# A linear-attention block with an MLP behind it: packets of two tokens for three loads, one chunk's inverse split by parity, and a new order of all steps

## The chip, the cores and the metric

The kernel runs on one core of one Trainium2 chip. The metric is the device time of the whole program in microseconds (us), the median over several runs; the profile is of one execution. The core has a tensor engine (PE, matrix products), a vector engine (DVE), a scalar engine (ACT), GpSimd (POOL) and SyncE (SP), which here only issues transfers. PEld in the profile is the loading of weights into PE.

## What is computed

```python
k_n = k / (np.linalg.norm(k, axis=-1, keepdims=True) + 1e-06)
for t in range(S):
    y[:, :, t] = einsum('bhd,bhde->bhe', q[:, :, t], state)
    v_old = einsum('bhde,bhd->bhe', state, k_n[:, :, t])
    state += beta[:, :, t] * einsum('bhd,bhe->bhde', k_n[:, :, t], v[:, :, t] - v_old)
x = y.transpose(0, 2, 1, 3).reshape(B, S, H * D)
xn = (x - mean(x)) / sqrt(var(x) + 1e-06) * g_ln
out = x + maximum(xn @ w_ch1, 0) @ w_ch2
```

There are 4 batches, 8 heads, 768 tokens and a head width of 48, all in FP32; the MLP goes from 384 to 1536 and back. The state starts at zero.

## The kernel before

**Tiling.** The 768 tokens are worked in 12 chunks of 64. Inside a chunk the recurrence is solved at once: the Gram matrix of the keys is made (`gram`, L786), a unit triangular matrix built from it and the norms is inverted, and the state is taken from chunk to chunk by `recur` (L967). Behind each chunk comes its part of the MLP (`mlp`, and for chunk 0 `by_halves`, L1313). The 32 heads of all batches stand side by side: two batches (index `e`) on the two halves of the 128 partitions, and the other index (`g`) and the heads in the free dimension.

**Chunk 0's inverse** (`first_inverse`, L648) is on PE and DVE, by doubling of blocks: after a first masked step, five steps, each a product E (L720), a masked copy on DVE (L727), a product Z (L737), transposes on DVE (L685) and copies on ACT (L679), for two groups of heads `g`. Then `recur(0)` makes u (product L996, scaled on DVE, L1001), y (L1020), the layer norm and its turn (L1092), and the MLP of chunk 0 begins (L1322).

**The other chunks' inverses** (`rows_inverse`, L822) are on DVE, row after row: for each row j one product of `n * w` elements (L856) and one subtraction (L863), with n = j + 1 and w = 31 - j, on blocks of 32 tokens. Chunk 1 stands alone on 64 partitions; later chunks go in pairs on 128. The Gram matrix goes to DRAM (`gd`) and comes back as rows (`gb`); the finished inverse goes by DRAM (`xd`) to `xts`. `join` (L879) puts two blocks of 32 together on PE.

**Loads.** `load_padded` (L445) reads queries of chunks 0 and 1 with one token of one head (48 numbers, 192 bytes) in a packet, into 64 columns per head of `tb[1]`; `load_raw` (L456) does so for keys, with the halves swapped for odd heads. `first_kt` (L561) turns 128x128 pieces with PE transposes (the profile names them L568) and copies them out on ACT (L573). `TURNED` (L225) says up to which chunk keys have swapped halves; `key_half` (L757) answers to it. The norms of a chunk are gathered as 4-byte packets of the Gram diagonal (`norms`, L920).

**Weights** come as 64-bit numbers through ACT's queue (`fetch`) and are made FP32 by ACT, DVE and POOL (`convert`, L514 to L542).

**Order.** Every step is put on a list by `add`; a table of numbers, `ORDER` (from L59), written out in full, says in which order they are issued. Each engine takes its steps strictly in that order, and so do the transfers on the SP and ACT queues among each other. A step waits on the semaphores of what it needs; all that stands behind it on its engine waits with it. A `z` in the table is a filler, a product of zeros by the unit matrix (L1511); `fill` (L553) issues wide products of zeros. The costs and due times that the calls of `add` carry have no effect on what is issued.

## Time and profile before

| | |
|---|---|
| median of 3 runs (lowest to highest) | 509.65 us (509.59 to 509.78) |
| the profiled execution | 506.83 us |
| its span, first to last instruction | 505.1 us |
| mean granted PE clock | 0.973 |
| packets on SP's queue | 189920, 40.58 MB |

A busy share says how much of the span an engine had an instruction in work. The clock is the share of full speed that PE was granted; here it is 0.50 or 1.00 for a few us at a time in the first 56 us and 1.00 from there to the end. Idle time before an instruction is put down to what ended it; "issue" means that nothing in the profile explains it. PE's waits before 48 us add up as the prediction tells; after that the longest is 0.4 us (L894, for DVE).

### The profile page before, as it was taken

The numbers are of one execution on the slowest core, as the hardware profiler recorded it, in microseconds if no ns is written. First come the engines' busy times: TensorE is split into PE (matmuls) and PEld (weight loads), VectorE is DVE, ScalarE is ACT, GpSimd is POOL, SyncE is SP. The second block draws the span as 40 slices with busy tenths as digits, with TensorE's granted clock in tenths as the row PEclk, the third lists the DMA queues.
The fourth block names the chain that finished last, engine by engine and source line by source line (L and its number), as shares of the span: only waits on it lengthen the run. The fifth ranks groups of instructions, "written<-read, shape, count | busy, mean of one in ns | idle before, by whom it ended". The sixth has DMA issues, their size and how long they took to land.

```text
span 505.1 us, 22184 instructions
## 1 busy us (share of the span) xinstructions
PE 485.9 (96%) x9606; PEld 445.7 (88%) x9606; DVE 355.2 (70%) x774; ACT 249.0 (49%) x620; POOL 275.7 (55%) x430
## 2 busy tenths in 40 slices
PE   6777999999999999999999999999999999999996
PEld 3666988688988898899999999999999999999996
DVE  9689987997699458886559898478899238143251
ACT  5777772633645434636444544436563347363230
POOL 5464527255754595629893462591642851645643
PEclk9776799999999999999999999999999999999999
DMA  8979896756646676448734434765245412111101
GB/s 173 308 153 187 270 189 79 107 138 133 90 87 106 192 127 114 46 100 205 155 41 64 102 55 153 150 91 87 57 85 136 82 23 58 43 50 46 31 12 31
DMA packets 196097, 54.99 MB, mean 109 GB/s; under 512 B 186076, under 2 KB 189404, under 8 KB 196000
## 3 DMA queue, kind: packets, MB, share of 16 engines
q1 hardware_dynamic: 189920, 40.58, 42.1%
q10 hardware_dynamic: 3872, 9.83, 6.1%
q0 software_dynamic: 2208, 3.17, 3.7%
q8 instruction: 75, 1.23, 1.0%
q14 instruction: 22, 0.18, 0.1%
HBM read 36.64 MB, written 16.91 MB: 106 GB/s over the span
## 4 chain that ended last, share of the span: by engine, by line
PE 78%; DVE 13%; SPq 3%; issue 2%; POOL 1%; DMA 1%; ACT 1%; ACTq 0%; DVEq 0%; POOLq 0%
PE f L1419 31%; PE f L1217 22%; PE f L1296 6%; DVE xb L863 4%; DVE tmp L856 4%; SPq L349 3%; PE by L1020 2%; PE two L1013 2%; PE by L979 2%; PE by L771 2%; PE two L979 2%; PE two L1030 1%; PE two L771 1%; PE by L894 1%; PE by L900 1%
## 5 line engine op out<-in xcount | busy, mean ns | idle before, releaser
L1406 POOL TENSOR_TENSOR h_all<-h_all 128x256 f32<-128x256 f32 x123 | 90.2, 746 | 133.3 <-PE f L1419 103.7
L1419 PE MATMUL f<-w_sb,h_all 128*128 128x192 f32 x492 | 109.5, 332 | 0.0
L1419 PE MATMUL f<-words,h_all 128*128 128x192 f32 x396 | 84.5, 330 | 0.3 <-POOL h_all L1406 0.3
L1419 PEld LDWEIGHTS f<-w_sb,h_all 128*128 128x128 f32 x492 | 81.8, 190 | 1.8 <-DVE o L1437 0.2
L863 DVE TENSOR_TENSOR xb<-xb,tmp 128x87 f32<-128x87 f32 (+21 forms) x186 | 73.7, 396 | 4.8
L856 DVE TENSOR_TENSOR tmp<-xb,gb 128x87 f32<-128x87 f32 (+21 forms) x186 | 73.1, 393 | 4.9
L1237 DVE TENSOR_TENSOR h_all<-h_all,f 128x512 f32<-128x512 f32 x96 | 63.6, 682 | 14.2 <-PE f L1217 13.1
L1419 PEld LDWEIGHTS f<-words,h_all 128*128 128x128 f32 x396 | 66.6, 190 | 1.7 <-POOL h_all L1406 1.0
L1296 PE MATMUL f<-xnt,w_sb 128*128 128x256 f32 x216 | 50.2, 382 | 0.0
L349 POOL DMA_DIRECT2D tb<-in_k_dram x64 | 41.9, 660 | 10.3 <-DVE kt L751 9.4
L1239 ACT ACTIVATE h_all<-h_all 128x512 f32<-128x512 f32 x48 | 28.5, 624 | 34.4 <-DVE h_all L1237 34.0
L1296 PEld LDWEIGHTS f<-xnt,w_sb 128*128 128x128 f32 x216 | 40.2, 190 | 5.2
L1233 ACT COPY h_all<-f 128x512 f32<-128x512 f32 x48 | 26.3, 590 | 33.9 <-PE f L1217 17.1
L1437 DVE TENSOR_TENSOR o<-f,x 128x192 f32<-128x192 f32 x33 | 11.6, 352 | 41.8 <-PE f L1419 25.9
L1217 PE MATMUL f<-words,w_sb 128*128 128x128 f32 x256 | 31.7, 276 | 0.0
L1305 ACT ACTIVATE h_all<-f 128x256 f32<-128x256 f32 x36 | 13.4, 383 | 34.8 <-PE f L1296 34.8
L1217 PEld LDWEIGHTS f<-words,w_sb 128*128 128x128 f32 x256 | 30.0, 192 | 0.2
L1217 PE MATMUL f<-xnt,w_sb 128*128 128x128 f32 x192 | 25.4, 276 | 0.0
L542 POOL TENSOR_TENSOR w_sb<-words 128x768 uint32<-128x768 uint32 (+1 forms) x11 | 15.0, 1364 | 17.7 <-DVE words L529 16.7
L1217 PEld LDWEIGHTS f<-xnt,w_sb 128*128 128x128 f32 x192 | 23.7, 192 | 0.1
L1322 PEld LDWEIGHTS f<-xnt,w_sb 128*128 128x128 f32 x144 | 19.5, 203 | 3.4 <-ACT h_all L1330 0.2
L1084 ACT ACTIVATE xnt<-xnt,g_sb 128x256 f32<-128x256 f32 x27 | 12.5, 499 | 19.2 <-DMA xnt<-xld 19.1
(246 smaller groups left out, 955.0 us busy)
## 6 DMA issues: line engine op xcount, KB each, us to landing
words<-in_moe_w_ch_dram ACTq DMA_DIRECT2D x10, 768.0 KB, 7.8
gd<-gsb SPq DMA_DIRECT2D x11, 512.0 KB, 3.9
v<-in_v_dram SPq DMA_DIRECT2D x24, 192.0 KB, 4.2
kr<-in_k_dram SPq DMA_DIRECT2D x46, 96.0 KB, 3.9
out_dram<-o SPq DMA_DIRECT2D x44, 96.0 KB, 2.4
xld<-xlt SPq DMA_DIRECT2D x9, 384.0 KB, 3.0
xnt<-xld SPq DMA_DIRECT2D x36, 96.0 KB, 3.3
gb<-gd SPq DMA_DIRECT2D x44, 64.0 KB, 3.0
```

The costliest lines, as they stand in the source:

```text
L349: add(eng, cost, lambda: QUEUE[eng].dma_start(out=out_, in_=in_), r, w, bulk=n * ns / 16e3, **kw)
L856: lambda j=j, n=n, w=w, t=t: nc.vector.tensor_tensor(out=t, in0=xv[:, 0:n, j : j + 1].to_broadcast([np_, n, w]), in1=gv[:, j : j + 1, j + ...
L863: "DVE", dve(n * w), lambda t=t, rest=rest: nc.vector.tensor_tensor(out=rest, in0=rest, in1=t, op=ALU.subtract),
L979: nc.tensor.matmul(dst[half(e), hp, j], src[drows(hp), (e if n else key_half(c, hp, e)) * GP + j], s_all[drows(hp), e, j], start=(n == 0 o ...
L1217: nc.tensor.matmul(wide(p[:, 128 * n : 128 * n + 128]), w[n // 2][:, n % 2 * 128 : n % 2 * 128 + 128], r, start=start and n == 0, stop=Tru ...
L1233: add("ACT", act(512), lambda: nc.scalar.copy(o, p), pk, ok)
L1237: add("DVE", dve(512), lambda: nc.vector.tensor_tensor(out=o, in0=o, in1=p, op=op), pk, ok)
L1239: add("ACT", act(512), lambda: nc.scalar.activation(o, o, ACTF.Relu), [], ok)
L1296: nc.tensor.matmul(p[:, 0:TOK], w1_sb[:, t, f * 128 : (f + 1) * 128], xnt[:, t], start=(t == 0), stop=(t == KC - 1))
L1322: nc.tensor.matmul(p[:, 0:128], w1_sb[:, t, f * 128 : (f + 1) * 128], xnt[:, t, cols], start=(t == 0), stop=(t == KC - 1))
L1406: add(eng, cost, lambda: e.tensor_tensor(out=out_, in0=x, in1=y, op=op), r, w, port=2 if eng == "Pool" else 1, pr=-2)
L1419: lambda f=f, t=start and f == 0: nc.tensor.matmul(p[:, 0:D2], lhs(f), rhs[:, f], start=t, stop=(f == F2 - 1), skip_group_check=True),
```

## The change

- **Packets of two tokens.** `load_pairs` reads queries of chunks 0 and 1 and keys of chunk 3 with two consecutive tokens of one head (96 numbers, 384 bytes) in a packet: 32 pairs on 32 partitions, the four batches on the four quarters, four transfers each.
- **Unit products.** `first_kt_pairs` turns them with plain products by the unit matrix: 64 columns of data as weights (16 of them belong to the next token or head and are not read later), 128 columns of the unit matrix streamed, 8 products for the even and 8 for the odd tokens. Copies on ACT put the two back in sequence, each writing every second element. Keys of chunk 3 so come without swapped halves, and `TURNED` goes from 4 to 3.
- **Parity.** `rows_inverse` takes `ways`; with 2, for chunk 1 only, even rows of the inverse are kept on partitions 0-63 and odd rows on 64-127. The gram rows are copied to the second half by one transfer (`gb.4`), beta is loaded twice, the diagonal is set by two POOL copies, and the results leave in 8 transfers instead of 4. Each row step then has n = j // 2 + 1.
- **Norms.** Chunk 1's norms, which `rows_inverse` has on its partitions, are turned by 8 small products and copied to `knrm`; the gather of the diagonal, a root on ACT and an addition on POOL go. For all chunks the reciprocal is written to `db_b` instead of over the norms.
- **Order.** The whole `ORDER` is new, over all 12 chunks, and has three fillers instead of one. At the start PE now issues three wide fills ahead of the first turn, and chunk 1's turns and Gram products and chunk 0's query turns ahead of the first E; a filler stands after E1 of group 0 and after Z1 and Z2 of group 1. DVE has six of its mask operations behind the first masked products. On SP the fourth load of gram rows stands behind three other loads, and the copy `gb.4` behind it.

The diff without the table `ORDER` (of 2992 entries before, 3004 after):

```diff
@@ -222,7 +222,7 @@
     FT = DFF // 128
     GH = 2 * H
     NP = H // 2
-    TURNED = 4
+    TURNED = 3
     LNPE = 2
     GP = 2 * NP
     FROM, LATER = 4, 6
@@ -280,7 +280,7 @@
     masks = [small[:, i].bitcast(I32) for i in range(6)]
     xor, bits, eye, brow = small[:, 6].bitcast(I32), small[:, 7].bitcast(I32), small[:, 8], small[:, 9]
     bnat = sb("bnat", [128, GH])
-    beta_f = sb("beta_f", [64, FB])
+    beta_f = sb("beta_f", [128, FB])
     beta_b = sb("beta_b", [128, NSL, BK])
     g_sb = sb("g_sb", [128, KC])
     eps = sb("eps", [128, 1])
@@ -361,7 +361,7 @@
         )
     for i in (2, 1):
         c_dve(
-            lambda i=i: nc.vector.memset(tb[i].rearrange("p (h d) -> p h d", d=DP)[:, :, D:], 0.0), 0.28, [("tbpad", i)],
+            lambda i=i: nc.vector.memset(tb[i][:, GH * D :], 0.0), 0.28, [("tbpad", i)],
         )
     c_dve(lambda: nc.vector.memset(nought, 0.0), 0.2, ["nought"], pr=-300)
     c_pool(lambda: nc.gpsimd.memset(ident, 0.0), 0.2, ["ident"])
@@ -442,11 +442,12 @@
     def nat(src, c, e):
         return src[2 * e : 2 * e + 2, :, c * C : (c + 1) * C, :].rearrange("g h p d -> p (g h) d")
 
-    def load_padded(i, src, c, engs, **kw):
-        for e in range(2):
+    def load_pairs(i, src, c, **kw):
+        for b in range(4):
             dma(
-                engs[e], tb[i].rearrange("p (h d) -> p h d", d=DP)[half(e), :, 0:D], nat(src, c, e),
-                GH * C, 16.5, [], [("tb", i, e, g) for g in range(2)], **kw,
+                "SP", tb[i][quad(b), 0 : GH * D].rearrange("p (h x) -> p h x", x=2 * D),
+                src[b, :, c * C : (c + 1) * C, :].rearrange("h (p u) d -> p h (u d)", u=2),
+                H * BK, 20, [("tbpad", i)], [("tb", i, b // 2, b % 2)], **kw,
             )
 
     def load_v(c, **kw):
@@ -571,6 +572,21 @@
             o = dst.rearrange("p (e g j) t -> p g j e t", e=2, g=2)[:, g]
             i = pair[g].rearrange("p (j e t) -> p j e t", j=NP, e=2)
             add("ACT", act(512), lambda o=o, i=i: nc.scalar.copy(o, i), pair[2 + g], [dkey + (g,)], **kw)
+
+    def first_kt_pairs(i, skeys, dst, dkey, pair, **kw):
+        for u in range(2):
+            ps, pk = pair[u], pair[2 + u]
+
+            def turn(u=u, ps=ps):
+                for j in range(NP):
+                    for hp in range(2):
+                        x0 = 2 * D * (2 * j + hp) + D * u
+                        nc.tensor.matmul(ps[half(hp), j * 128 : (j + 1) * 128], tb[i][:, x0 : x0 + DP], ident)
+            add("PE", 0.9, turn, skeys + ["ident"], pk, np=16, arr=0.9, **kw)
+        for u in range(2):
+            o = dst.rearrange("p (b j) (t u) -> p u j b t", b=4, u=2)[:, u]
+            v = pair[u].rearrange("p (j b t) -> p j b t", j=NP, b=4)
+            add("ACT", act(512), lambda o=o, v=v: nc.scalar.copy(o, v), pair[2 + u], [dkey + (g,) for g in range(2)], **kw)
 
     def first_beta(pair, **kw):
         def turn():
@@ -819,35 +835,57 @@
                 for b in range(C // L):
                     yield ((cc * 2 + e) * (C // L) + b) * GH, c, slice(e * C + b * L, e * C + b * L + L), slice(b * L, b * L + L)
 
-    def rows_inverse(L, chunks, beta_l, xd, **kw):
-        np_ = C * len(chunks)
-        gv, xv, tv = gb[0:np_], xb[0:np_], tmp[0:np_]
+    def rows_inverse(L, chunks, beta_l, xd, ways=1, **kw):
+        own = C * len(chunks)
+        np_, LA = own * ways, L // ways
+        gv, xv, tv = gb[0:np_], xb[0:np_, 0:LA], tmp[0:np_]
         gbk = [("gb", n) for n in range(8)]
         nb, ns = GH * L, 13.7
-        add("Pool", 0.1 + 0.85e-3 * L * L, lambda: nc.gpsimd.memset(xv, 0.0), [], ["xb"], after=MASK_SCRATCH, **kw)
+        add("Pool", 0.1 + 0.85e-3 * L * LA, lambda: nc.gpsimd.memset(xv, 0.0), [], ["xb"], after=MASK_SCRATCH, **kw)
         for n, (p0, c, rows, cols) in enumerate(spots(L, chunks)):
             dma(
                 "SP", gv[p0 : p0 + GH], gds[c % NG][rows, :, cols].rearrange("s h t -> h s t"),
                 nb, ns, [("gd", c % NG)], [("gb", n)], **kw,
             )
+        if ways > 1:
+            dma("SP", gb[own:np_], gb[0:own], own, 168, [("gb", n) for n in range(4)], [("gb", 4)], **kw)
         diag = lambda t: t.rearrange("p s t -> p (s t)")[:, 0 :: L + 1]
         nrm, db = nrm_b[0:np_], db_b[0:np_]
         add("ACT", 0.25, lambda: nc.scalar.sqrt(nrm, diag(gv)), gbk, ["nrm_b"], **kw)
         add("DVE", 0.15, lambda: nc.vector.tensor_scalar_add(nrm, nrm, 1e-6), [], ["nrm_b"], port=2, **kw)
-        add("DVE", 0.35, lambda: nc.vector.reciprocal(nrm, nrm), [], ["nrm_b"], port=2, **kw)
-        add("DVE", 0.2, lambda: nc.vector.tensor_tensor(out=db, in0=nrm, in1=nrm, op=ALU.mult), ["nrm_b"], ["db_b"], port=1, **kw)
+        add("DVE", 0.35, lambda: nc.vector.reciprocal(db, nrm), ["nrm_b"], ["db_b"], port=2, **kw)
+        add("DVE", 0.2, lambda: nc.vector.tensor_tensor(out=db, in0=db, in1=db, op=ALU.mult), [], ["db_b"], port=1, **kw)
         add(
             "DVE", 0.2, lambda: nc.vector.tensor_tensor(out=db, in0=db, in1=beta_l[0], op=ALU.mult),
             beta_l[1], ["db_b"], port=1, **kw,
         )
-        add("Pool", 0.25, lambda: nc.gpsimd.tensor_copy(out=diag(xv), in_=db), ["db_b"], ["xb"], **kw)
+        for q in range(ways):
+            pq = slice(own * q, own * q + own)
+            add(
+                "Pool", 0.25,
+                lambda q=q, pq=pq: nc.gpsimd.tensor_copy(
+                    out=xv[pq].rearrange("p s t -> p (s t)")[:, q :: L + ways], in_=db[pq, q::ways]
+                ),
+                ["db_b"], ["xb"], **kw,
+            )
+        if ways > 1:
+            i, ps, pk = chunks[0] % 2, f_[3][:, 0:GH], FK[3]
+
+            def turn():
+                for e in range(2):
+                    for b in range(2):
+                        nc.tensor.matmul(
+                            ps[quad(2 * e + b)], nrm_b[quad(e)], ident[quad(e), BK * e + GH * b : BK * e + GH * b + GH]
+                        )
+            add("PE", 0.13, turn, ["nrm_b", "ident"], pk, np=8, arr=0.02, **kw)
+            add("ACT", 0.21, lambda: nc.scalar.copy(knrm[i], ps), pk, [("kn", i, n) for n in range(2)], **kw)
         add(
             "DVE", dve(L * L),
             lambda: nc.vector.tensor_tensor(out=gv, in0=gv, in1=db[:, None, :].to_broadcast([np_, L, L]), op=ALU.mult),
             ["db_b"], gbk, port=1, **kw,
         )
         for j in range(L - 1):
-            n, w = j + 1, L - 1 - j
+            n, w = j // ways + 1, L - 1 - j
 
             t = tv[:, 0 : n * w].rearrange("p (s t) -> p s t", t=w)
             rest = xv[:, 0:n, j + 1 : L]
@@ -863,13 +901,16 @@
                 "DVE", dve(n * w), lambda t=t, rest=rest: nc.vector.tensor_tensor(out=rest, in0=rest, in1=t, op=ALU.subtract),
                 ["tmp"], ["xb"], port=1, **kw,
             )
-        xdv = xds[xd][0:np_]
-        dma("SP", xdv, xv, np_, 25 + L * L * 0.15, ["xb"], [("xd", xd)], **kw)
+        xdv = xds[xd][0:np_, 0:LA]
+        dma("SP", xdv, xv, np_, 25 + L * LA * 0.15, ["xb"], [("xd", xd)], **kw)
         for n, (p0, c, rows, cols) in enumerate(spots(L, chunks)):
-            dma(
-                "SP", xts[c % NX][rows, :, cols], xdv[p0 : p0 + GH].rearrange("h s t -> s h t"),
-                nb, ns, [("xd", xd), ("xz", c % NX)], [("xq", c % NX, n % 4)], **kw, cap=cap(chunks[0] // 2 - 1) if chunks[0] > 1 else None,
-            )
+            for q in range(ways):
+                dma(
+                    "SP", xts[c % NX][rows.start + q : rows.stop : ways, :, cols],
+                    xdv[own * q + p0 : own * q + p0 + GH].rearrange("h s t -> s h t"),
+                    nb // ways, ns, [("xd", xd), ("xz", c % NX)], [("xq", c % NX, n % 4 + 4 * q)], **kw,
+                    cap=cap(chunks[0] // 2 - 1) if chunks[0] > 1 else None,
+                )
 
     def xt_keys(c):
         return [("xq", c % NX, n) for n in range(8)] + [("xz", c % NX)] + [
@@ -1497,8 +1538,14 @@
             beta[2 * e : 2 * e + 2, :, C : 2 * C].rearrange("g h (b t) -> b (g h) t", t=FB),
             GH * C // FB, 11, w=[("beta_f", e)], pr=-85,
         )
+    for e in range(2):
+        dma(
+            "ACT", beta_f[C + e * FB : C + (e + 1) * FB],
+            beta[2 * e : 2 * e + 2, :, C : 2 * C].rearrange("g h (b t) -> b (g h) t", t=FB),
+            GH * C // FB, 11, w=[("beta_f", 2 + e)], pr=-54, t0=20.0,
+        )
     dma("Pool", g_sb, g_ln.rearrange("(t p) -> p t", p=128), 384, 10, w=["g_sb"], pr=-84)
-    load_padded(1, q, 0, ("SP", "SP"), pr=-100)
+    load_pairs(1, q, 0, pr=-100)
     for e in range(2):
         dma("Pool", brow[BK * e : BK * e + GH], beta[2 * e : 2 * e + 2, :, 0:C].rearrange("g h t -> (g h) t"), GH, 20, w=[("brow", e)], **chain)
     load_v(0, pr=-79)
@@ -1520,7 +1567,7 @@
     first_g(order, **chain)
     first_kt(kraws[1], raw_keys(1), kts[1], ("kt", 1), PAIRS[3], pr=-97)
     gram(1, PAIRS[3], halves=True, pr=-97)
-    first_kt(tb[1], tb_nat(1), qts[0], ("qt", 0), PAIRS[3], pr=-99)
+    first_kt_pairs(1, tb_nat(1), qts[0], ("qt", 0), PAIRS[3], pr=-99)
     first_inverse(order, **chain)
     queries(0, PAIRS[3], halves=True, pr=-100)
     first_swaps(pr=-80)
@@ -1534,7 +1581,7 @@
 
     c_pool(lambda: nc.gpsimd.memset(xts[1], 0.0), 1.0, [("xz", 1)], pr=-20)
     c_pool(lambda: nc.gpsimd.memset(tb[0], 0.0), 1.0, [("tbpad", 0)], t0=30.0)
-    rows_inverse(FB, (1,), (beta_f, [("beta_f", e) for e in range(2)]), 1, pr=-20)
+    rows_inverse(FB, (1,), (beta_f, [("beta_f", e) for e in range(4)]), 1, ways=2, pr=-20)
     def prep_g(m):
         pr = 20 * m - 15
         for c in (2 * m, 2 * m + 1):
@@ -1544,8 +1591,8 @@
                 first_kt(kraws[2], raw_keys(2), *kt, PAIRS[3], pr=pr, t0=40.0)
             elif c == 3:
                 keys = [("tb", 2, e, hp) for hp in range(2) for e in range(2)]
-                load_raw(c, dst=tb[2], keys=keys, pr=pr, t0=29.0)
-                first_kt(tb[2], keys + [("tbpad", 2)], *kt, PAIRS[3], pr=pr, t0=40.0)
+                load_pairs(2, k, c, pr=pr, t0=29.0)
+                first_kt_pairs(2, keys + [("tbpad", 2)], *kt, PAIRS[3], pr=pr, t0=40.0)
             else:
                 load_blocks(2 * (c % 2), k, c, "Pool", pr=pr, t0={2: 80.0, 3: 120.0}.get(m, 40.0 * m - 20))
                 turned(c, 2 * (c % 2), *kt, pr=pr)
@@ -1590,11 +1637,11 @@
             join(c, pr=pr, lag=0.5)
         recur(c, pr, lag=0.8)
 
-    load_padded(1, q, 1, ("SP", "SP"), pr=8.2, t0=42.0)
+    load_pairs(1, q, 1, pr=8.2, t0=42.0)
     load_v(1, pr=8.1, t0=42.0)
-    norms(1, pr=4)
+    scale_v(1, knrm[1], [("kn", 1, n) for n in range(2)], pr=4)
     join(1, pr=3)
-    first_kt(tb[1], tb_nat(1), qts[1], ("qt", 1), PAIRS[0], pr=4)
+    first_kt_pairs(1, tb_nat(1), qts[1], ("qt", 1), PAIRS[0], pr=4)
     queries(1, pr=4)
     recur(1, 10, lag=0.5)
     for e in range(2):
```

6 lines of the change are left out of this document (5 added, 1 removed), and 180 rows, old and new, of the table ORDER.

## Prediction

> **What bounds the kernel now.** I read the page's busy shares first, then the busy times by stretch, then the chain of work, then the waits of the tensor engine (PE).
>
> ```profile
> PE 485.9 (96%) x9606; PEld 445.7 (88%) x9606; DVE 355.2 (70%) x774; ACT 249.0 (49%) x620; POOL 275.7 (55%) x430
> ```
>
> PE is busy 96% of the span. The stretches, cut where the granted clock changes, show where the rest is (columns: PE, weight loads, DVE, ACT, POOL, clock, DMA, GB/s):
>
> ```profile
> 11.20:14.70 3.50, 2.32 (x98) 1.76 (x96) 3.32 (x7) 3.18 (x10) 0.00 (x0) 1.00 1.38 217
> 14.70:21.50 6.80, 5.69 (x128) 5.08 (x132) 3.23 (x8) 5.05 (x11) 2.94 (x4) 0.50 0.98 352
> 21.50:24.90 3.40, 0.99 (x61) 0.86 (x57) 2.95 (x6) 2.30 (x6) 2.45 (x5) 0.99 0.87 276
> 24.90:31.60 6.70, 5.85 (x172) 4.89 (x166) 4.64 (x10) 5.41 (x14) 3.49 (x4) 0.50 0.71 125
> 31.60:42.00 10.40, 6.96 (x264) 5.67 (x264) 9.80 (x26) 6.68 (x17) 5.75 (x7) 0.99 0.95 250
> 42.00:48.40 6.40, 4.54 (x128) 4.11 (x132) 5.36 (x17) 4.77 (x12) 4.30 (x5) 0.50 1.02 134
> 48.40:55.70 7.30, 7.27 (x155) 6.69 (x147) 7.16 (x14) 5.70 (x15) 4.41 (x4) 0.50 0.72 199
> 55.70:490.00 434.30, 433.62 (x8492) 402.48 (x8492) 305.88 (x648) 210.53 (x528) 239.45 (x375) 1.00 0.50 99
> ```
>
> From 48.4 us PE never rests: of 434.3 us only 0.7 are idle. So an edit there is worth only the PE work that it adds or takes away; relief of DVE, ACT, POOL or the DMA queues is worth nothing by itself. What can be won lies before 48.4, where PE idles some 14 us, and in the half clock (0.50), which lasts in steps of about 3.4 us (6.8, 6.7, 13.7). The last step hurts most: 7.3 us of dense work at half speed cost 3.6 us.
>
> The chain of work through the start:
>
> ```profile
> 18.16 1.90 PE f L568 x8
> 20.06 1.06 PE by L737 x32
> 21.12 0.71 PE two L720 x32
> 21.83 0.34 PE f L771 x21
> 22.17 2.41 issue
> 24.58 0.39 PE f L771 x10
> ```
>
> It is chunk 0's inverse: a product (L720), a masked copy on DVE (L727), a product (L737), transposes on DVE (L685), five times over for two head groups. Between its steps stand query turns (L568, 1.90) and query products (L771), with a stall of 2.41 us that no engine explains.
>
> **The change, part by part.** Times go against this execution: 506.83 us, of which 505.1 are the span and 1.7 lie around it. The median of the timed runs, 509.65, is 2.8 higher; I work out a difference and put it on the median.
>
> *Packets.* Queries of chunks 0 and 1 and keys of chunk 3 go from 2048 packets of 192 bytes to 1024 of 384 each; the norm gather of chunk 1 (2048 packets of 4 bytes) goes. The page's SP queue row gives 42.1% of 16 engines over 505.1 us for 189920 packets, 17.9 ns each. So 3072 + 2048 packets are up to 5.7 us of all 16 engines; if a packet of twice the length costs twice, 2.3 us. Value on the clock: zero directly, because no PE wait after the first keys is on a transfer. What it may buy is the 2.41 us stall, since the DMA engines are full there (0.98). I take half of it, bounds 0 to 2.41. The four query issues instead of two cost SP about 1.3 us; SP then sits 7.7 us waiting for the gram copies, which hides them. The two added beta loads on ACT's queue (0.37 each) fall into ACT's wait for the first keys (2.18).
>
> *Parity.* The rows of chunk 1's inverse are dealt to 128 partitions. The products of lengths add up to 2856 instead of 5456 elements, twice; rows of 60 and 256 elements (0.21 and 0.42 us) give 1.07 ns an element, so DVE saves 5.6 us. DVE is full from 35 to 72 us, but PE waits for it after 48.4 only at 123 us (L894, 0.4, and 0.3 of issue beside it): I take 0.3, bounds 0 to 0.7. Four more stores (0.5 us of SP each) come 5.6 us earlier than before and stay covered.
>
> *Unit products.* A turn of 8 transposes takes 0.97 us in the dense stretch (1.04 with the last one's end). It becomes 16 products of 128x64 weights against 128 columns. Nearest from one side: L1217, 96 products of 128x128 in 10.72 us, 0.112 each, so 1.8 us, 0.8 more. From the other: L771's 64 products on column halves in turn, 1.16 us for 64 columns each, 0.018, a third of half of 0.112, so halves do overlap; with two at a time, 0.9 us and nothing lost. Two of the three uses are in the dense stretch. The tile with column halves is the nearer row, so I take 0.25 each, bounds 0 and 1.0 each. The norm turn (8 small products; L579's took 0.30) adds 0.2. Together +0.7. The copies out write every second element: same count, taken at no cost, up to 0.56 each on ACT, which has room.
>
> A rule speaks against this part. The Trainium skill, "TensorE: Matmul & The Clock Gate", section Terms, says that transpose mode is four times faster for FP32; by it the two uses would cost 13.5 us more. The trace has transposes at 0.121 and products at 0.112 for the same 128x128, so it does not agree.
>
> *Order of the start.* Step by step by hand, with durations of the rows. **To the second step:** three fills end at 1.64 + 3.38 + 1.02 = 6.0, when the first keys land (5.93). The norm chain, a dozen DVE operations of 0.17 and five of 0.7 bring group 0's first product (13.47 before) to about 15.1; chunk 1's gram and the query turns now run in that wait. The second step's product (20.89 before) then comes at about 21.4, because DVE now serves both groups by turns: +0.5. **Second to fifth step of group 0:** 19.2 us before (20.89 to 40.10). The new DVE order puts group 0 first: I add 13.4 us of products at 0.7, masked copies at 0.73, transposes at 0.43 and the conversions between. To this come half the stall (1.2) and, as eight PE steps cost 1.1 instead of 0.7 at half clock, half of 3.2: 16.2, so -3.0. The two added fillers (1.2 us at half clock) stand where the next product waits for DVE (0.71 and 0.87) and are meant as half hidden in that. **Fifth step to the first u (L1001):** the rows of chunk 1 before it shrink by 2.5, but conversions (+1.45) and six mask operations (+1.1, part of them earlier) come in: +0.8. Start: -1.7, bounds -3.3 (no stall, no half clock) and +1.5 (all of both).
>
> *Clock of the dense stretch.* One step of 3.4 less at half clock is 1.7 us. Full 128-row products of chunk 3's keys now stand before the first MLP products, where before 64-row tiles and transposes stood; I take half a step, -0.9, bounds -3.4 and +1.7. The same page, Part 4, says that transposes do not count as busy for this gate; by it the whole step would be won and the sum be 0.8 lower. The trace is divided: the clock came up at 21.5 after a step with 1.90 us of transposes in it.
>
> **Sum:** -1.7 - 0.9 + 0.7 - 0.3 = -2.2; 509.65 - 2.2 = 507.4.
>
> **The rivals.**
>
> *Nothing in sum, 509.6.* The products run one after another (+2.0 instead of +0.5) and the start wins 1 less: for it that the hand count rests on stalls that may stay, against it the overlap in L771.
>
> *Slower, 511.8: the second half of the gram rows comes too late.* SP copies partitions 0-63 to 64-127 only when all four block loads have landed, one transfer behind another where before there was none. Before, the gram's store took 7.0 us to be seen (SP's wait), the loads went out from 23.63 to 27.7. After: store at 13.1, loads from 20.1, three other loads between, last block out at 26.1. With the median landing of 3.0 the copy is there at 32.1; with 7 each, as the query loads took (7.2), at 40.1. DVE's norm steps stand before a transpose of the fourth step (about 33.3, or 36 with stalls), and ACT's root before two of its copies. Beyond 36 everything of group 0 waits: +4.4. SP meanwhile holds the keys of chunk 2 and queries of chunk 1 behind the waiting copy. For it: DMA share 0.71 to 1.02 in these stretches; against it: the lower packet count and the gram's earlier start.
>
> *Much slower, 520.9:* unit products at four times a transpose's time, 0.48 us each, 7.7 instead of 0.97 a turn, +13.5 for two. L1217's 0.112 speaks against it. This is the skill's rule above.
>
> **From this to the numbers.** A difference under 0.2% (1.0 us) can't be told from none. Forecast 507.4: 0.53. Nothing: 0.11. Slower by the late copy: 0.33. Four-fold products: 0.03. The forecast's own range is 504 to 509; the start's better bound with the clock's reaches 503, the late copy with serial products 513. The case of nothing is 0.10 within the bound and 0.01 beyond it. Faster 0.53, within 0.2% 0.10, slower 0.37.
>
> **What would show it.** In the profile after: PE without rest from about 46.5 instead of 48.4; no issue stall above 1 us before that; clock 1.00 before 54; L568's successor at about 1.2 us a turn at full clock; the first u of DVE near 45.5; ACT's L835 successor waiting for the copied gram less than 1 us; PE idle after 60 us under 1 us. It is wrong if DVE or ACT wait for gb past 36 us, if the stall comes back elsewhere, if the half clock reaches further into the MLP, or if the new order leaves PE idle later.

## The result

| | before | after |
|---|---|---|
| median of 5 runs (lowest to highest) | 509.59 us (507.45 to 509.78) | 513.41 us (511.91 to 514.39) |
| the profiled execution | 506.83 us | 514.39 us |
| its span | 505.1 us | 512.4 us |
| mean granted PE clock | 0.973 | 0.978 |
| packets on SP's queue | 189920 | 185040 |

The change makes the kernel slower: ratio 1.0088, 95% interval 1.0066 to 1.0110, that is 3.8 us by the medians. The two profiled executions lie 7.3 us apart in their spans: that of before lay below its timed runs, that of after is its slowest. Their difference shows where the time goes, the medians how much it is. Ratios leave disturbed runs out and go by the runs of before taken together with each version (medians 508.25 to 509.59), so a ratio need not be that of two medians in the tables.

The busy shares and the stretches of after, cut where its granted clock changes and where the MLP begins (PE, weight loads, DVE, ACT, POOL, clock, DMA, GB/s):

```profile
PE 485.3 (95%) x9690; PEld 445.8 (87%) x9690; DVE 342.4 (67%) x774; ACT 247.4 (48%) x620; POOL 277.5 (54%) x430
```

```profile
11.20:21.50 10.30, 7.12 (x248) 5.66 (x239) 8.34 (x26) 8.91 (x21) 1.15 (x2) 1.00 1.01 350
21.50:32.70 11.20, 6.53 (x298) 5.29 (x292) 7.20 (x17) 8.82 (x22) 8.47 (x12) 1.00 0.97 215
32.70:42.20 9.50, 3.16 (x93) 2.59 (x84) 3.33 (x7) 2.70 (x6) 4.28 (x6) 0.50 0.85 228
42.20:53.20 11.00, 9.06 (x243) 8.35 (x243) 10.08 (x25) 8.36 (x20) 7.95 (x8) 0.50 0.69 157
53.20:60.90 7.70, 6.38 (x235) 5.42 (x227) 7.19 (x22) 5.46 (x14) 3.66 (x5) 1.00 0.80 190
60.90:500.00 439.10, 436.67 (x8475) 405.71 (x8468) 299.47 (x648) 207.26 (x525) 240.76 (x377) 1.00 0.48 95
```

DVE has 12.8 us less to do, 9.1 of it in the row steps, where the parity was to save 5.6; PE has as much to do as before. The row from 32.70 to 42.20 is new: every compute engine is idle for more than half of it, PE works 3.2 of 9.5 us, and the clock is at half until 53.2. The first MLP product comes at 60.92 us (before: 53.14), and from there to the end it takes 451.5 us (before: 452.0). So all of the loss lies ahead of the MLP. The chain of work says where:

```profile
13.21 5.35 DMA gd<-gsb
...
21.22 2.89 SPq L349
24.11 0.04 issue
24.16 0.91 SPq L349
25.07 0.04 issue
25.11 8.99 DMA gb<-gd
34.12 8.09 DMA gb<-gb
42.21 0.02 issue
42.24 0.04 issue
42.29 0.27 ACT nrm_b L854
```

The gram rows go to DRAM at 13.21; the fourth load goes out at 25.11, behind three other loads, and lands 8.99 us later; the copy to the second half takes 8.09 more. ACT has stood at its root (L854) since 36.9, and behind it, on ACT and DVE, stand copies and a transpose that belong to chunk 0 and have nothing to do with the gram rows (columns: start, duration, instruction, the idle time before it and what ended it):

```profile
36.69 0.26 ACT L695 COPY xt<-by 64x128 f32<-64x128 f32 x1
42.29 0.26 ACT L854 ACTIVATE nrm_b<-gb 128x32 f32<-128x32 f32 x1 [5.35 <-DMA tb<-in_k_dram]
42.57 0.26 ACT L695 COPY xt<-f 64x128 f32<-64x128 f32 x1
```

The row of the root puts its wait down to keys of chunk 3 (`tb`). The root reads only `gb`, though, and the semaphore of the copy, landed at 42.21, is what it waited for, as the chain above has it.

PE's waits in the first 60 us (total, times, longest) show who pays:

```profile
PE by L736 <- ACT xt L695: 9.0, 3, 6.7
PE f L787 <- issue: 1.3, 1, 1.3
```

The wait of 6.7 us ends at 43.05, when the copy of line 695 has run. It is the product of group 1's fourth step. Group 0's fifth (43.96) stands behind it on PE, and the transpose that this one needs came on DVE only at 43.52, behind the norm steps.

### The profile page after: what moved, and what is told of

Its sections match the earlier page's. It is cut to its first block, busy times and chain, and to the rows that moved or that the text cites. A ratio compares the mean times of both kernels' runs of the same rounds, so it can differ in the third digit from the quotient of the medians.

```text
span 512.4 us, 22352 instructions
## 1 busy us (share of the span) xinstructions
PE 485.3 (95%) x9690; PEld 445.8 (87%) x9690; DVE 342.4 (67%) x774; ACT 247.4 (48%) x620; POOL 277.5 (54%) x430
## 3 DMA queue, kind: packets, MB, share of 16 engines
q1 hardware_dynamic: 185040, 40.84, 40.9%
q8 instruction: 76, 1.25, 1.1%
## 4 chain that ended last, share of the span: by engine, by line
PE 81%; DMA 6%; POOL 4%; SPq 3%; DVE 2%; ACT 2%; issue 2%; ACTq 0%; DVEq 0%; POOLq 0%
PE f L1460 28%; PE f L1258 19%; PE f L1337 9%; PE f L1363 3%; PE f L1378 3%; SPq L349 3%; PE by L1061 2%; PE by L1020 2%; PE two L1020 2%; PE two L1054 2%; PE by L787 2%; DMA gb<-gd 2%; DMA gb<-gb 2%; PE two L787 1%; PE two L1071 1%
## 5 line engine op out<-in xcount | busy, mean ns | idle before, releaser
L1460 PE MATMUL f<-w_sb,h_all 128*128 128x192 f32 x492 | 108.2, 331 | 0.9 <-DVE o L1478 0.9
L894 DVE TENSOR_TENSOR tmp<-xb,gb 128x87 f32<-128x87 f32 (+23 forms) x186 | 69.4, 373 | 5.1
L901 DVE TENSOR_TENSOR xb<-xb,tmp 128x87 f32<-128x87 f32 (+23 forms) x186 | 68.3, 367 | 4.8
L1099 ACT ACTIVATE x<-by 128x384 f32<-128x384 f32 x23 | 11.1, 484 | 29.4 <-DVE o L1478 15.2
```

Of the source, the lines that this page charges most:

```text
L894: lambda j=j, n=n, w=w, t=t: nc.vector.tensor_tensor(out=t, in0=xv[:, 0:n, j : j + 1].to_broadcast([np_, n, w]), in1=gv[:, j : j + 1, j + ...
L901: "DVE", dve(n * w), lambda t=t, rest=rest: nc.vector.tensor_tensor(out=rest, in0=rest, in1=t, op=ALU.subtract),
L1460: lambda f=f, t=start and f == 0: nc.tensor.matmul(p[:, 0:D2], lhs(f), rhs[:, f], start=t, stop=(f == F2 - 1), skip_group_check=True),
```

## The experiments

Theories at the outset. **A:** the late copy holds ACT and DVE, which take their work in order, and with them chunk 0's inverse. **B:** not the copy, but the full transfer engines: everything issued between 20 and 45 us lands late. **C:** the unit products run one after another, 1 us more a turn. D and F came up on the way: **D:** the new order has stalls of its own. **F:** PE waits for its own instructions. All runs, with the first product of chunk 0's MLP and the time from there to the end of the profiled execution:

| run | median us | ratio to before, 95% interval | first MLP product | rest |
|---|---|---|---|---|
| (before) | 509.59 | | 53.14 | 452.0 |
| (after) | 513.41 | 1.0088 [1.0066, 1.0110] | 60.92 | 451.5 |
| direct | 510.37 | 1.0032 [1.0007, 1.0058] | 57.75 | 448.7 |
| gbfirst | 510.96 | 1.0051 [1.0024, 1.0079] | 58.80 | 449.9 |
| latenorms | 513.71 | 1.0100 [1.0059, 1.0142] | 62.37 | 449.6 |
| nopackets | 518.13 | 1.0154 [1.0110, 1.0198] | 55.75 | 458.3 |
| noparity | 514.77 | 1.0129 [1.0087, 1.0171] | 55.98 | 455.7 |
| direct2 | 512.37 | 1.0062 [1.0035, 1.0089] | 58.76 | 448.9 |
| packets | 519.46 | 1.0236 [1.0165, 1.0307] | 52.72 | 464.1 |
| orderonly | 519.24 | 1.0222 [1.0156, 1.0288] | 57.55 | 457.2 |
| before_shift | 522.30 | 1.0275 [1.0223, 1.0327] | 53.50 | 469.1 |
| packets_shift | 511.71 | 1.0071 [1.0042, 1.0099] | 54.92 | 455.9 |
| order_shift | 517.09 | 1.0180 [1.0142, 1.0218] | 59.99 | 454.3 |
| gbwords | 511.71 | 1.0070 [1.0040, 1.0099] | 58.49 | 453.5 |
| gbsp | 511.18 | 1.0032 [1.0010, 1.0055] | 59.69 | 448.4 |
| gbsp_q0 | 513.08 | 1.0078 [1.0050, 1.0105] | 61.66 | 449.3 |
| before_s24 | 508.74 | 0.9996 [0.9972, 1.0019] | 53.38 | 452.5 |
| direct_s24 | 512.23 | 1.0056 [1.0033, 1.0080] | 61.68 | 449.1 |

### Is it the copy? direct, gbfirst, latenorms

```diff
 # direct: rows_inverse, the second half from DRAM, no transfer behind another
-dma("SP", gb[own:np_], gb[0:own], ...)
+for p0, c, rows, cols in spots(L, chunks):
+    nc.sync.dma_start(out=gb[own + p0 : own + p0 + GH], in_=gds[c % NG][rows, :, cols].rearrange("s h t -> h s t"))
 # gbfirst: order on SP
-gb.3 gb.1 gb.2 kr tb v gb.0 gb.4 tb beta_b
+gb.3 gb.1 gb.2 gb.0 gb.4 kr tb v tb beta_b
 # latenorms: the root, the norms and the scaled rows (steps 256-280) moved behind chunk 0's u and y
```

> The changed kernel, with the copy of the gram rows to partitions 64-127 (issued at 34.1 us, landed at 42.2, when the four block loads had landed) replaced by four block loads from DRAM, which wait for none of the others. Theory A, that the chain of two transfers holds ACT's root and behind it group 0's inverse for 6.7 us: the root runs at 34 to 37 us, PE's wait of 6.7 falls below 1.5, and the median falls by 4 to 6 us to about 508. Theory B, that the transfer engines are full and anything in that place lands late: the four loads land as late as the copy did (40 us or later), the wait moves little, and the median stays within 1.5 us of 513.4. Theory C, that the loss is PE work (unit products at 0.12 us each) and stalls of issue after 55 us: the median stays at 512 or above whatever the wait does.

> The changed kernel with the fourth block load and the copy moved, on SP's queue alone, directly behind the third block load, ahead of half of chunk 2's keys, a quarter of chunk 3's and half of chunk 0's values. Theory A (place in the queue): the fourth load goes out at 20.5 instead of 25.1 us, the copy at about 25, the root no longer waits (before 33), and the median falls by 4 to 6 us, unless what now stands behind the waiting copy is late: values of chunk 0 (needed for the first u), then PE waits for u instead. Theory B (full engines): the copy still takes 8 to 9 us to land and goes out after a load that took 9, so the root waits until about 38, and half of the gain at most is seen. Theory C: 512 or above.

> The changed kernel with its transfers as they are, but the steps that wait for the copied gram rows (the root on ACT, the norm steps on DVE and POOL, the norm turn, the first rows) moved in their engines' order behind the first y of chunk 0 and behind the first part of the layer norm; the norm turn takes another PSUM bank. Theory A in its in-order form (what costs is that ACT and DVE stand still behind the late rows, not that the rows are late): the wait of 6.7 goes though the copy still lands at about 42, and the median falls by 4 to 6 us. If rows that are late cost as such (chunk 1's inverse becomes late), the gain at the start is given back at the first join, with PE waiting there for DVE. Theory C: 512 or above.

Measured: against after's ratio direct wins back 0.56%, 2.9 us, and gbfirst 0.37%, 1.9 us; the MLP begins 3.2 and 2.1 us earlier than in after. Latenorms takes the wait of 6.7 away and wins nothing: PE then waits 4.2 us for chunk 2's keys and 2.3 for u. SP issued these keys at 40.40, when an earlier load of chunk 3's keys had landed, 2.9 us after the copy. So A holds in place: ACT's order passes the late rows on to chunk 0. It is not the whole, though, and neither edit brought the root forward as A had it. In gbfirst the copy is there at 31.20, but other steps ahead of the root on ACT are late, and it runs at 39.57. In direct the last of the four loads lands only at 39.63, nearly as late as B had it, and the root runs at 40.05.

### One part alone: nopackets, noparity, packets, orderonly, and one more repair: direct2

```diff
 # nopackets: after, with the loads and transposes of before (192-byte packets, TURNED = 4)
 # noparity: after, with rows_inverse as before for chunk 1 (no copy, 64 partitions)
-rows_inverse(FB, (1,), ..., 1, ways=2, pr=-20)
+rows_inverse(FB, (1,), ..., 1, pr=-20)
 # packets: before, in its order, with load_pairs and first_kt_pairs
-first_kt(tb[1], tb_nat(1), qts[0], ("qt", 0), PAIRS[3])
+first_kt_pairs(1, tb_nat(1), qts[0], ("qt", 0), PAIRS[3])
 # orderonly: nopackets and noparity together
 # direct2: direct, and all eight loads in a row on SP
-gb.3 gb.1 gb.2 kr tb v gb.0 (four loads of the second half)
+gb.3 gb.1 gb.2 gb.0 (four loads of the second half) kr tb v
```

> The changed kernel with the packets of two tokens and the unit products undone: loads of 192 bytes and PE transposes as before, in the new order (two of the four steps of each query load issue nothing). Theory C, PE work: a unit-product turn took 1.97 us against 0.97 for the transposes, two of them after the start, so the median falls by 2 us to about 511.4. Theory A: the same fall of 2 us and no more, the wait of 6.7 stays or grows a little, since 3072 more packets go out. Theory B: with 3072 more packets (3.4 us of all 16 engines at 17.9 ns each) everything lands later, the wait grows by 2 us or more, and the median does not fall.

> The changed kernel without the parity split: chunk 1's inverse is done whole on 64 partitions again, so there is no copy of the gram rows, and the four extra stores go; two-token packets, unit products, norms from the blocks and the new order stay. Theory A (the copy makes the root of ACT late, and all of group 0's inverse waits behind it): the root comes 5 us or more earlier than the 42.3 of the changed kernel, PE's wait for ACT in its L736 products falls from 6.7 us to under 3, the first MLP products come 3 us or more earlier than 60.9, and the time is 3 to 5 us below the changed kernel, 508.5 to 510.5. Theory B (the full transfer engines, not the copy as such): the four loads land late all the same, the root stays after 38, and the time falls by less than 2. In both the rows of chunk 1 take 5.6 us more of DVE; if that relief was worth what I forecast, it costs 0.3.

> The changed kernel with two edits: the second half of the gram rows is loaded straight from DRAM by four loads, as in the run direct, and these and the fourth load stand right behind the third on SP, as in the run gbfirst. Theory A (a chain of one transfer behind another, held behind three other loads): root before 36, PE's waits for ACT before 45 us under 3 us in all, first MLP products before 57, time at or below direct, 506.5 to 509.5. Theory B (the engines are full from 25 to 41 us whoever asks): the eight loads still need 8 to 9 us each to land, root at 38 or later, time within 1 us of direct's 510.4.

> The kernel before, in its old order, with two-token packets and unit products alone (queries of chunks 0 and 1, keys of chunk 3); two ACT copies stand one place earlier, since both parts are needed at once. My forecast's terms for this part: unit products +0.25 each in the dense stretch, half of the 2.41 us stall won: 0.7 us below the kernel before. Theory C (the products run one after another, 1.97 instead of 0.97 a turn, and the stall has nothing to do with the packets): 2 us above the kernel before, each of the two turns in the dense stretch at 1.9 to 2.0 us at full clock.

> The changed kernel with neither packets nor parity: what is left is the new order of all steps, the two more fillers, and the norms of chunk 1 from the blocks. My forecast's terms: start -1.7, clock -0.9, norm turn +0.2, so 2.4 us below the kernel before. Theory A says the same within 1.5 us, since the copy is gone. Theory D (the new order brings stalls of PE without a cause in the profile, as the run nopackets showed): 1 to 6 us above the kernel before, with PE stalls put down to issue of over 1 us after 60 us.

Measured: without the copy (noparity) the root runs at 38.00 and the MLP begins 4.9 us earlier, nearly as A said; and yet the time doesn't fall. The rows, in which DVE has 5.3 us more to do than in after, now end last. PE's waits and the place in its timeline:

```profile
PE f L1369 <- ACT h_all L1377: 3.0, 1, 3.0
```

```profile
74.19 0.94 PE L1369 MATMUL f<-xnt,w_sb 128*128 128x128 f32 x6 [2.97 <-ACT h_all L1377]
```

ACT itself waited 4.59 us for DVE's layer norm, which stood behind the rows until 72.9; the clock then fell to half for 6.8 us. In the new order the parity's relief is needed; the copy is its price.

Direct2 issues all eight loads by 25.4 and has them by 28.1, but loses 3.9 us at 22 to 26 in another wait of PE, for a transpose on DVE that waits for copies on ACT. These stand behind the issue of a beta load, which waited until 23.83 for an earlier weight fetch to land (why is told with gbwords below). The engines are full (a DMA share of 0.95 from 20 to 40 us), and it looks as if who goes first only chooses who waits; that is argued.

Nopackets still has the copy, behind the same loads, and yet its MLP begins 5.2 us earlier than after's, where B had the wait grow. Its root, and PE's waits for ACT:

```profile
38.03 0.26 ACT L859 ACTIVATE nrm_b<-gb 128x32 f32<-128x32 f32 x1
```

```profile
PE by L741 <- ACT xt L700: 3.3, 3, 1.9
```

The fourth load and the copy landed after 6.30 and 5.91 us there, and after 7.20 and 5.96 in latenorms, whose transfers are those of after; in after it was 8.99 and 8.09. So the place of the copy alone doesn't make a wait of 6.7 us. The slow landings in after's profiled execution, its slowest, belong to it, and why they were so slow stays open.

The surprise was in the times of the other three. Packets alone, which I had put at -0.7, and the order alone, at -2.4, each cost 10 us by the medians, 11 to 12 by the ratios; undoing the packets made the changed kernel slower. The first MLP product of packets comes earlier than before's. PE's waits in packets have a releaser that no engine explains, one of them at 20 us, three behind the first MLP product:

```profile
PE two L746 <- issue: 3.7, 1, 3.7
PE f L920 <- issue: 2.8, 1, 2.8
...
PE two L1005 <- issue: 1.4, 1, 1.4
...
PE f L926 <- issue: 1.3, 1, 1.3
```

### What "issue" is: before_shift, packets_shift, order_shift, before_s24

The page's table of queues has a row of its own for instructions (packets, MB, share of the engines; here that of packets):

```profile
q8 instruction: 76, 1.25, 1.0%
```

In the trace these are single packets of 16384 bytes, spread over the whole run: 75 in before, for 19,343 records of PE (matmuls, weight loads and 131 others), one for 258. I set PE's stalls against these packets and counted all PE records up to the end of each stall:

```
kernel        packet of instructions   stall of PE       PE records up to its end, modulo 256
before         22.35 -  23.22           22.17 -  24.58    705     193
after          63.23 -  64.18           64.05 -  65.52   2497     193
nopackets      59.78 -  60.72           59.57 -  62.39   2497     193
packets       146.62 - 147.93          147.77 - 149.20   6081     193
packets       201.68 - 202.98          201.64 - 204.46   8385     193
before_shift  147.17 - 148.40          148.43 - 149.92   6081     193
before_shift  205.53 - 206.66          205.46 - 208.01   8385     193
before_shift  221.67 - 222.59          221.77 - 224.19   8897     193
```

The last two columns are the whole of it: a stall of this kind ends only where a block of 256 PE instructions begins, and 1.3 to 1.7 us after the packet of that block has ended. The same holds for all 41 waits of 0.7 us or more that the 18 traces put down to issue: each ends within three records of such a border. In before the packet starts up to 5.4 us after PE has entered the block ahead in the first 60 us, where the engines are full, and behind 60 us half of the packets start 0.6 to 1.4 us after it (median 0.85); it takes 0.9 to 1.7 (median 1.04). With the 1.5 us behind the packet that makes about 3.4 us, an estimate: a block that PE leaves sooner can end in a wait. Which stretches of work make up a block depends only on how many PE instructions stand ahead. Unit products are 48 instructions more a turn (64 records instead of 16), 144 in three. That is theory F, and it can be tried with nothing but empty products at the start, where PE waits for the first keys:

```diff
 # before_shift, packets_shift (37 tiny products, 144 instructions more), order_shift (45, 176 more)
-fill(1, 512, f_[3], FK[3])                 # the first of three wide fills
+for _ in range(37):
+    nc.tensor.matmul(ps[0:32, 0:8], nought[0:32, 0:32], nought[0:32, 0:1].to_broadcast([32, 8]))
 # before_s24: all three wide fills kept, 6 tiny products (24 instructions) added
```

> The kernel before with one of its first wide fills (1.7 us of zeros) replaced by 37 tiny products of zeros, so that 144 more PE instructions stand ahead of everything else; nothing else is changed. Theory F (PE's instructions come by transfers of 256 of them; a block that PE runs through in less than about 3.4 us ends in a wait for the next): the trace of before, cut into blocks of 256 shifted by 144, has blocks of under 3.4 us that end near 146, 198, 209, 311, 353, 387 and 430 us of that trace, by 0.8 to 1.7 us each, so PE stalls put down to issue appear there, and the time is 5 to 11 us above the kernel before. Any theory without instruction blocks: the extra products lie in PE's wait for the first keys, and the time is within 1 us of the kernel before.

> The run packets (the kernel before with two-token packets and unit products alone) with the same edit as in before_shift: 144 more PE instructions ahead of everything, in place of one wide fill. The unit products themselves are 144 more PE instructions in all; with both, the blocks of 256 stand 32 further on than in the kernel before, where its trace has no block under 3.4 us. Theory F: the stalls of packets near 148, 202, 217 and 364 us go, and the time falls from 519.5 by 6 or more, to 509 to 513; what is left above the kernel before is the cost of the unit products themselves, 2 us if they run one after another in the dense stretch (theory C). Without instruction blocks: 519 to 521, as packets.

> The run orderonly (the new order without packets and parity) with 176 more PE instructions ahead of everything, 45 tiny products in place of one wide fill. In orderonly's trace, cut into blocks shifted by 176, no block takes under 3.4 us. Theory F: the stalls near 142, 218 and 363 us go, and the time falls from 519.2 by 5 or more, to 510 to 514; what stays above the kernel before is then the start and the waits of DVE (theory A has this order waiting for the parity's relief). Without instruction blocks: 518 to 521.

> The kernel before with 6 tiny products of zeros added behind one of its first wide fills: 24 more PE instructions (0.2 us) ahead of everything, in PE's wait for the first keys. The converse of before_shift: by the trace of before, cut into blocks of 256 shifted by 24, no block in the dense stretch takes under 3.4 us, while with none added four do, by 0.2 to 1.3 us. Theory F: no loss, and a gain of 0.5 to 2.5 us if the timed runs fall into those four waits more often than the profiled one. If the tiny products themselves made before_shift slow: slower by 1 or more.

Measured: by the medians the same 144 instructions make before 14.0 us slower and packets 7.8 us faster; 24 change nothing. The empty products themselves so cost nothing. Of the ten blocks that the cut of before's trace had marked as under 3.4 us, three end in a stall in before_shift (the waits for numbers 23, 32 and 34); the later seven, of which the expectation names four, don't. In these seven the packet started between 1.2 us before PE's entry into the block and 0.2 after it, in the three 0.8 to 2.1 after it; what decides when it starts stays open. PE's waits from 60 us on, and three stretches around the stalls:

```profile
PE f L896 <- issue: 2.5, 1, 2.5
PE f L902 <- issue: 2.4, 1, 2.4
PE f L1421 <- DVE rstd L965: 1.8, 1, 1.8
PE two L981 <- issue: 1.5, 1, 1.5
```

```profile
148.40:156.20 7.80, 6.30 (x50) 5.32 (x49) 5.65 (x12) 0.60 (x2) 0.71 (x2) 0.57 0.19 37
...
205.00:214.30 9.30, 6.76 (x83) 5.48 (x79) 6.80 (x16) 1.90 (x7) 0.36 (x1) 0.63 0.39 66
...
221.50:228.00 6.50, 4.09 (x49) 3.35 (x38) 4.43 (x9) 0.46 (x3) 2.14 (x4) 0.74 0.34 50
```

Each is dear because the clock falls to half behind it: 0.57 over 7.8 us are 6.7 us at half, 0.63 over 9.3 are 6.9, 0.74 over 6.5 are 3.4; half of these 17.0 is 8.5, and with the stalls (6.4) 14.9, against 14.0 by the medians. Without the shift the same stretches of before run at 1.00.

Packets_shift gives what the packets cost when no stall falls behind 60 us: 1.0071, 3.6 us. Two turns in the dense stretch are 2.0 of it, and the first MLP product comes 1.8 later; two stalls of 1.82 and 2.50 stand ahead of it, where before has one of 2.41. Order_shift fell by 2.2 only: the stalls behind 60 us went, others came before 50 (2.05, 1.48 and 1.43 us), and PE waits 4.6 us for h_all behind DVE's rows, as in noparity.

### What stands behind the copy: gbwords, gbsp, gbsp_q0, direct_s24

```diff
 # gbwords: gbfirst, and two conversions of weights on ACT (steps 244, 246) moved behind group 0's copies
 # gbsp: gbwords, and two weight fetches put out by SP
-dma("ACT", dst, src, 256, 115, w=WORD_KEYS[BUF[i]])
+dma("SP" if i in (6, 7) else "ACT", dst, src, 256, 115, w=WORD_KEYS[BUF[i]])
 # gbsp_q0: gbsp, with queries of chunk 1 and keys of chunk 3 as before, and 128 PE instructions ahead
 # direct_s24: direct, with 6 tiny products (24 instructions) ahead
```

> The run gbfirst (the fourth load of gram rows and the copy right behind the third on SP) with one more move: the two conversions of a weight piece on ACT (the ones that waited 4.03 us for their transfer in gbfirst, ahead of four copies for group 0's inverse and of the root) stand behind those copies. Theory A2 (what holds group 0 after the copy comes in time is ACT, which waits in order for weights): PE's wait of 3.0 us for ACT's copy in the fourth step goes, the first MLP products come 3 us earlier than gbfirst's 58.8, and the time falls by 2 to 4 us, to 507 to 509. Rival: another wait stands right behind it (DVE or POOL for the same weights), and the time stays within 1 us of gbfirst's 511.0.

> The run gbwords with two weight fetches (768 KB each) put out by SP instead of ACT, at the same places of the order. In gbfirst and gbwords ACT stood 4.0 and 5.2 us at such an issue while copies for group 0's fourth step waited behind it. Theory A3 (an issue on ACT's queue holds ACT while the transfer engines are full, and ACT's copies with it): PE's wait for ACT before the second product of the fourth step (2.2 us) and the DVE wait of 3.3 us go, the root comes at 36 to 37 instead of 39.8, the first MLP products 2.5 to 4 us earlier than gbwords' 58.5, and the time is 2 to 4 us below gbwords, 508 to 510. Rival B (the engines are full; who issues makes no difference, since SP then holds the keys of chunk 2 and the beta loads behind the same wait): PE waits for kr or v instead, as in latenorms (4.2 us), and the time is within 1 us of gbwords' 511.7 or above.

> The kernel of gbsp with the queries of chunk 1 and the keys of chunk 3 loaded and turned as in the kernel before (192-byte packets, transposes); only chunk 0's queries keep two tokens in a packet and unit products. The 96 PE instructions that this takes away, and 32 more, are put back ahead of everything as 33 tiny products in place of one wide fill, so that no block of 256 in the dense stretch is under 3.4 us by gbwords' trace. Theory C (a unit turn costs 1.97 instead of 0.97 us in the dense stretch, all of it on the path): 2 us below gbsp in the same batch. My forecast's 0.25 each: 0.5 below. If the two-token packets relieve the full engines at 25 to 45 us, the two loads of 2048 instead of 1024 packets make the start later, and the gain is under 1 or none.

> The run direct (second half of the gram rows loaded straight from DRAM) with the same 24 more PE instructions ahead. By its trace one shift of 24 leaves no block under 3.4 us; with none there are a few, 1.8 us in all. Theory F: 0.5 to 2 us below direct's 510.4, which would be level with the kernel before or 1 us above it; what then remains is the 2 us of the two unit turns, less what the new order gains. Without instruction blocks: direct's ratio to the kernel before, 1.003, again.

Measured: gbwords' MLP begins only 0.3 us earlier than gbfirst's, for a reason that its timeline shows (ACTq and SPq are issues of transfers):

```profile
26.50 0.60 SPq L357 DMA_DIRECT2D kr<-in_k_dram  x1
...
31.56 0.26 ACT L703 COPY xt<-f 64x128 f32<-64x128 f32 x1
36.50 0.43 ACTq L357 DMA_DIRECT2D words<-in_moe_w_ch_dram  x1
36.97 0.27 ACT L703 COPY xt<-f 128x128 f32<-128x128 f32 x1 [5.16 <-DMA kr<-in_k_dram]
```

Not a conversion, but the issue of a weight fetch holds ACT for 4.7 us, with chunk 0's copy behind it, though POOL had freed the two buffers by 32.7. My theory was that full engines hold an issue. The last line names another cause, keys of chunk 2, and the trace's semaphores bear it out: transfers of SP and ACT share eight semaphores, and an issue waits until the transfer that had its semaphore before has landed. The fetch at 36.50 has the one of the keys that SP issued at 26.50, whose last packet landed at 36.42. In gbfirst a fetch at 36.39 has that of values issued at 27.13 and landed at 36.31. Gbwords also has a stall of 2.57 us for instructions at 61.6, with 3.4 us at half clock behind it; its rest is 3.6 us longer than gbfirst's.

In gbsp, where SP issues it, that wait is gone, the root runs at 36.72 as forecast, and the first u comes at 49.02 instead of 51.45. But the MLP doesn't begin earlier: between 51 and 59 us a stall for instructions (1.00) and a half clock until 58.0 instead of 51.6, with a unit turn of 3.15 instead of 2.03, give it back. By the ratio gbsp is 1.9 us better than gbwords, level with direct; gbwords' stall at 61.6 may be most of that. Gbsp_q0 was meant to win the two unit turns back and lost 1.9 by the medians instead: a turn does cost 1.09 instead of 1.97, but PE lost 2.1 us at 36 in a stall for instructions, PE waited 1.9 for chunk 2's keys, and the MLP begins 2.0 later. Direct_s24 missed: no stall behind 60 us was there to be won, and its start came 3.9 us later than direct's in the profiled run. Why the start of one order differs so much between runs stays open; the packets of instructions, which then wait up to 5 us, are one reason in the traces, and the landing of the gram rows is another. No version here beats the kernel before.

## Why the prediction was wrong

**The step that failed** is "Second to fifth step of group 0: -3.0". The rival "the second half of the gram rows comes too late" had its place and its mechanism, and I gave it 0.33; its price was 4.4 us, and PE's wait is 6.65. By the trace of after: second step at 21.65 (forecast 21.4), fifth at 43.96. The 22.3 us between are 6.65 of one wait and 15.7 of the rest, for which I had counted 16.2 by hand. Fifth step to first u: 8.6 (7.6 forecast). What decided was the landing time. I had it at 3.0, the median over the run, and at 7 from the query loads of that stretch; it was 8.99 and 8.09 in this execution. The median comes mostly from stretches with half-full engines (DMA 0.50 from 55.70 on in before); in those from 11 to 42 us it was 0.71 to 1.38. The row of the same stretch was the right one, and it put the copy past 36.

**Unit products, +0.5 for two, were +2.0.** The turn before and after, both in the dense stretch at full clock:

```profile
60.73 1.04 PE L568 MATMUL two<-ident,tb 128*128 128x128 f32 x8
```

```profile
66.46 1.97 PE L584 MATMUL two<-ident,tb 128*64 128x128 f32 x32
```

Eight transposes are 8 records, 16 products are 32: an FP32 product is two records, a transpose one. I had read the counts of L1217 and L771 as products; they are records, so a product there costs twice what I took. The overlap that I hoped for is there: in the records the two column halves start 0.007 us apart and a pair comes every 0.109 us; 16 pairs make 1.75, and the end of the last one the rest. The Trainium skill, "TensorE: Matmul & The Clock Gate", section Terms, has transpose mode four times faster for FP32; I had set it aside on the same miscount. Its direction was right: for the same 128x128 data two products on column halves take 0.218 us and a transpose 0.109, by the starts of their records, so a transpose is two times faster here, not four.

With these two sizes the sum is 507.4 + 4.4 (the rival's price) + 1.5 = 513.3; measured were 513.4. That it comes out so near is partly luck: it has the rival's price in place of the 6.65, and in the profiled run the first u alone comes at 52.57 where I had said near 45.5. The bounds of the start don't follow from its terms either: without stall and half clock the hand count gives -4.5, not -3.3, and with all of both +1.1, not +1.5.

**Half of the 2.41 us stall to the packets' credit** was wrong in kind. The stall is the wait for the second packet of instructions, which started 5.4 us after PE had entered the block ahead. After has 1.25 at 26.05 in its place and 1.47 at 65.52; that the first is about half of 2.41 is luck.

**Parity, -0.3,** was worked out in the old order and says nothing of the new one, where PE without it loses 3.0 us and then has 6.8 at half clock. **Clock, -0.9,** came out near in its number, not for its reason: the half clock ends at 53.2, the MLP begins at full clock, and the 2.6 us of it that before has at half are won, 1.3 us. But the MLP also begins 7.8 us later, so this doesn't show that the products of chunk 3's keys did it. **SP's covered issues** held: no PE wait is on a store. **PE past 60 us:** 2.4 us idle where I had said under 1, of it 1.5 for instructions and 0.9 for DVE.

The parts don't add: against before the packets alone cost 3.6 us and the order alone 8.8 (both with shifted blocks), all three together 3.8. A sum of terms from the old order's trace was the wrong form for a new table of steps, in which one part's wait is hidden or laid open by another part.

## What to carry to other kernels

A transfer that waits for another one, on a queue and ahead of an in-order engine's other work, is to be priced with the landing times of its own stretch, not with the median of the run. Before a wait at an issue is put down to full engines, look which transfer had its semaphore before. Before a count in a trace is used as a price, divide it by the calls in the code: an FP32 product shows as two records, a transpose as one. And when an edit changes the number of PE instructions early on, move the blocks back with empty products before judging it: here the same edit is worth +10 or +3.6 us.

## What the runs showed of the hardware

- **PE's instructions come by transfer while it runs**, 256 at a time, by the same engines as the data; behind 60 us a border reached too early cost 1.3 to 2.8 us in packets and before_shift, and in five cases of six 3.4 or 6.8 us at half clock behind it. The Trainium skill, "Trainium Architecture — The Big Picture", section The software stack, has the instruction streams brought to each engine when the program is loaded; by the 75 packets between 14 and 484 us of before most of PE's come later.
- **An issue holds its engine until its semaphore is free**: ACT stood 4.7 us in gbwords and 3.6 in gbfirst, until 0.08 us after the last landing of an SP transfer with the same semaphore. That full engines hold an issue by themselves, no run shows.
- **Landing is longer where the engines are full, and varies**: in after 64 KB took 8.99 us and 256 KB 8.09 at a DMA share of 0.93 and 0.84, where the median over the run of before is 3.0 for the 64 KB loads. In nopackets and latenorms the same two transfers took 6.30 and 7.20, 5.91 and 5.96.
